# Four time units of slack before a K table's matmul set, in the list schedule of a gated mix kernel

## The chip, the cores and the metric

The kernel runs on one core of a Trainium2 chip. TensorE (PE in the profile) multiplies matrices into PSUM, VectorE (DVE) and ScalarE (ACT) do elementwise work, GpSimd (POOL) and SyncE (SP) mostly issue DMAs. The metric is the device time of one execution in microseconds; lower is better. Every engine works through its own instructions in the order in which the program issues them, and waits at an instruction whose inputs are not there yet.

## The reference

For a sequence u of 2048 tokens with 512 channels, two branches are mixed with a gate per token. Branch A is a long convolution whose kernel K is a sum of 128 complex exponentials per channel; branch B is a bilinear GLU with 1792 hidden units.

```python
g = sigmoid((x * gate_w).sum(-1, keepdims=True))            # x = A_u, [1, 2048, 512]
# A: state-space convolution
P = exp((A * dt[:, None])[:, :, None] * pos[None, None, :]) # [512, 128, 2048]
K = 2.0 * einsum("dn,dnl->dl", C, P).real                   # [512, 2048]
y = irfft(rfft(u_t, 2 * L) * rfft(K, 2 * L), 2 * L)[:, :, :L]
a = y + u * D_skip
# B: bilinear GLU
b = einsum("bsf,fd->bsd", (x @ w_gate) * (x @ w_up), w_down)
out = g * a + (1 - g) * b
```

## The kernel before

The whole computation is written as small tasks that are collected by `work.add` (L198) and then put in order by `Work.run` (L268), a list scheduler. A task has an engine, an expected duration in units of a microsecond, the tiles it reads and writes, a rank, and, for sets of many small matmuls, a value `many`. `Work.inputs` (L227) gives the time at which a task's inputs are there by the plan: the latest planned end of the tasks that it depends on, plus a small lag. `slots` (L236) adds the wait for a free buffer. `run` then picks, again and again, the task with the smallest (start, rank, number) over all engines, fixes its planned start and end, and goes on. The plan's times are used for the order only: on the chip each engine takes its instructions in this order and waits by semaphores for what it needs. Two sets with `many` are planned to start no nearer than `APART` = 6 units (or `LESS` = 4, for the last two groups' transforms) after the end of the set before (L186, L294, L306).

Three streams share the engines.

- The GLU (`glu`, L650). 14 hidden tiles in four groups, over four token tiles of 512. Each product is done with three matmuls (high and low parts), as tasks of three matmuls of 128x512 (`product`, L540, `down`, L583). They have rank 2, the lowest, and fill TensorE wherever nothing else is ready. In the profile they are the matmuls into `pg`, `pu` and `y`.
- The K tables (`phases`, `direct_powers`, `leads`, `x_table`, `v_table`, L892 to L1034). The 512 channels go in 16 blocks of 32. For each block VectorE and ScalarE build an X table (two buffers) and a V table (one buffer) of powers of the complex exponentials. `k_block` (L1041) multiplies them on TensorE in one set of 128 small matmuls (`kgen`, the matmuls `k<-v,x`), which ScalarE and VectorE then fold into the tile `kt`. This set, called a K set below, has rank 0 and `many` = `APART`. The next block's V table may be written only when the K set has read this one.
- The convolution by Fourier transforms. After every fourth block (b % 4 == 3) `k_first` (L1072) transforms the K of 128 channels, one of four groups, and `transforms` (L1338) does the second stage, the product with the transformed u, the inverse and the last stage (`m_second`, `m_product`, `m_inverse`, `m_last`), through DRAM buffers between the stages. Stores of the transformed K (`sk_d`) and of the inverse (`y_d`) are issued on SP's queue, the loads that follow the first on POOL's. All these stages are sets with `many` too. The last group's transforms are what the end of the kernel waits for, beside the last GLU matmuls.

The main loop (L1381) adds, for each block b, the phases of block b + 1, the V table of b, the powers and the X table of b + 1, and the K set of b; the scheduler orders them as it finds them ready.

Of the kernel before, what the change touches and what calls it, by code (L numbers as in the profile page):

```python
# [20 lines left out]
KT = D // P  # L21
# [148 lines left out]
class Work:  # L170
# [24 lines left out]
    def memory(self):  # L195
        return Tile(self, None, None, None, None, None, False)

    def add(self, engine, us, fn, r=(), w=(), rank=1, after=0.0, dma=0, hold=(), rows=(), many=0):  # L198


        task = Task(len(self.tasks), engine, us, fn, rank, after, dma)
        task.rows, task.many = rows, many
        self.tasks.append(task)
        clash = lambda p, q: p is None or q is None or p == q
        split = lambda x: x if isinstance(x, tuple) else (x, None)
        for tile, part in map(split, r):
            task.deps.update(t for p, t in tile.writers if clash(p, part))
        for tile, part in map(split, w):
            task.deps.update(t for p, t in tile.writers + tile.readers if clash(p, part))
        for tile, part in map(split, r):  # L210
            tile.readers.append((part, task))
        for tile, part in map(split, w):
            tile.writers.append((part, task))
        for tile, _ in map(split, [*r, *w, *hold]):
            if tile.pool and tile not in task.tiles:
                task.tiles.append(tile)
                tile.users.append(task)
        task.deps.discard(task)
        return task
# [7 lines left out]
    def inputs(self, task):  # L227

        at = task.after
        for d in task.deps:  # L230
            if d.end is None:
                return None
            at = max(at, self.ready(task, d))
        return at

    def slots(self, task, at):  # L236

# [87 lines left out]
def gated_mix_kernel(  # L325
# [16 lines left out]
    pe, dve, act, sp, pool_q = (InOrder(tc, e) for e in (nc.tensor, nc.vector, nc.scalar, nc.sync, nc.gpsimd))  # L342
    uv = u.rearrange("(p r) d -> p r d", r=NR)
    ov = out.rearrange("(p r) d -> p r d", r=NR)
    work = Work()
    add = work.add
# [12 lines left out]
    m_su, m_sk, m_y, m_out, m_xs, m_turn = (work.memory() for _ in range(6))  # L359
# [5 lines left out]
    def new(pool, tag, shape, dtype=F32, bufs=1, loose=False):  # L365
        return work.tile(pools[pool], tag, shape, dtype, bufs, loose)

    def bank():
        return new("ps_k", "k", [P, D], bufs=4, loose=True)
# [5 lines left out]
    def stage(shape):  # L375
        return new("mid", "ts", shape, bufs=2, loose=True)
# [23 lines left out]
    def power_sets():  # L400
        for k in range(NP):
            pool_q.memset(turns[:, k : k + 1], float(TURNS[k]))

    add("dve", 0.5, memsets, w=[m_const, m_skip], rank=0)
    add("pool", 4.0, power_sets, w=[m_powers], rank=0)


    raws = {}

    def load(key, src, rank=0):  # L410
        if key in raws:
            return
        t = raws[key] = new("glu", "raw", [P, D], bufs=2)
        add("sp", 0.42, lambda: sp.dma_start(t.t, src), w=[t], dma=256, rank=rank)
# [35 lines left out]
    ws, wd, xs = {}, {}, {}  # L450
# [522 lines left out]
    def x_table(b):  # L973

        x, ri, (su, di) = xtab[b], ris[b], sus[b]
        ps = new("tab", "ps", [P, TB, 4])
        lead = [(x, ("l", k)) for k in range(3)]
        tt(0.26, lambda: ps.t, lambda: x.t[:, 0, :, 0:4], lambda: x.t[:, 1, :, 0:4], ALU.add, lead, [ps])
        outer(
            x, lambda: x.t[:, :, :, 0:4], lambda: ps.t, lambda: ri.t[:, :, :, W_M],  # L980
            lambda: su.t[:, :, W_M], lambda: di.t[:, :, 4:11], [*lead, ps, ri, su, di],
        )
        return x
# [54 lines left out]
    def apart_of(q):  # L1038
        return work.LESS if q >= KT - 2 else work.APART

    def k_block(b, x, v):  # L1041
        pk = bank()

        def kgen():
            pv = pk.t.rearrange("p (g j) -> p g j", j=64)
            for d in range(TB):
                ch, g = d % 4, d // 4
                for c in range(2):
                    pe.matmul(
                        pv[32 * ch : 32 * ch + 32, g, :], x.t[:, c, d, :], v.t[:, c, d, :], start=c == 0, stop=c == 1,  # L1050
                        tile_position=(0, 32 * ch),
                    )

        if b % 4 == 0:
            kts["now"] = new("tab", "kt", [P, 2, 2, 32, 16])
        kt, g0 = kts["now"], b % 4 * 8
        add("pe", 2.15, kgen, r=[x, v], w=[pk], rank=0, hold=[kt], many=work.APART)
        pv = lambda a: pk.t.rearrange("p (g a b k) -> p g a b k", a=2, b=2, k=16)[:, :, a]
        side = lambda h: kt.t[:, h, :, g0 : g0 + 8].rearrange("p b g k -> p g b k")
        add("act", 0.37, lambda: act.copy(side(1), pv(0)[:, :, :, ::-1]), r=[pk], w=[(kt, (1, b % 4))])  # L1060
        for h, op in enumerate((ALU.add, ALU.subtract)):
            add(
                "dve", 0.42, lambda h=h, op=op: dve.tensor_tensor(out=side(h), in0=pv(1), in1=side(1), op=op),
                r=[pk, (kt, (1, b % 4))], w=[(kt, (h, b % 4))], rank=0,
            )
        if b % 4 == 3:
            k_first(b // 4, kt)
# [48 lines left out]
    def evict(q, n, us, to, src, r, w):  # L1116

        if q == KT - 1 and n % 2:
            add("dve", us + 0.1, lambda: dve.tensor_copy(to(), src()), r=r, w=w)
        else:  # L1120
            add("act", us, lambda: act.copy(to(), src()), r=r, w=w)
# [92 lines left out]
    def m_inverse(q, T0, ys, ws):  # L1214


        banks, shape = [bank() for _ in range(4)], [P, 2, 2, 2, P]
        if q == KT - 1 and T0:
            sts = [new("tab", n, shape) for n in ("ri", "e")]
        else:  # L1220
            sts = [stage(shape) for _ in range(2)]

        def fn():
            for t in range(2):
                for i in range(2):
                    cs, to = slice(P * i, P * i + P), slice(P * (2 * t + i), P * (2 * t + i) + P)
                    for k in range(2):
                        for e in range(2):
                            for j in range(4):
                                lanes = slice(32 * j, 32 * j + 32)  # L1230
                                pe.matmul(
                                    banks[j].t[64 * e : 64 * e + 64, to], ws[t].t[lanes, i, e, k],
                                    ys[t].t[lanes, k, e, cs], start=k == 0, stop=k == 1, tile_position=(32 * j, 64 * e),
                                )

        add("pe", 2.13, fn, r=[*ys, *ws], w=[*banks, (m_turn, (q, T0))], rank=1, hold=sts, many=apart_of(q))
        for j in range(4):
            st, m = sts[j // 2], j % 2
            evict(
                q, j, 0.6, lambda st=st, m=m: st.t[:, :, :, m],  # L1240
                lambda j=j: banks[j].t.rearrange("p (t i d) -> p t i d", t=2, i=2), [banks[j]], [(st, m)],
            )
        for h in range(2):
            st = sts[h]
            for p in range(2):
                b0 = 32 * (T0 + p) + 16 * h
                add(
                    "sp", 0.42,
                    lambda b0=b0, st=st, p=p: sp.dma_start(
                        y_d[q, b0 : b0 + 16].rearrange("(u e) n d -> (e n) u d", u=8),  # L1250
                        st.t[p::2].rearrange("p t i j d -> p (t i j) d"),
                    ),
                    r=[st], w=[(m_y, (q, T0 + h, p))], dma=256,
                )
# [125 lines left out]
    x = x_table(0)  # L1380
    for b in range(NB):  # L1381
        if b + 1 < NB:
            if b % 2 == 0:
                amplitudes([n for n in (b + 1, b + 2) if n < NB])
            phases(b + 1)
        v, old = v_table(b), x
        if b + 1 < NB:
            direct_powers(b + 1)
            leads(b + 1)
            x = x_table(b + 1)  # L1390
        k_block(b, old, v)
        if b % 4 == 3:
            transforms(b // 4)
# [56 lines left out]
```

## Time and profile before

| | |
|---|---|
| three runs | 592.37, 589.72, 591.31 us; median 591.31 |
| the profiled execution | 588.79 us, its span 587.0 us |
| TensorE | 575.0 us busy, 98% of the span |
| VectorE | 511.7 us, 87% |
| ScalarE | 401.3 us, 68% |
| GpSimd | 113.8 us, 19% |
| the 16 K sets | 2048 matmuls, 33.0 us of TensorE |

The profile is of one execution. A row of a timeline gives the start in us from the span's beginning, the time taken, the engine, the line (here always that of the helper that issues), the operation, the tile written and the tiles read, how many instructions were merged into the row, and in brackets the engine's idle time before it with what ended it. A row of the waits gives who waited for whom, the total in us, how often, and the longest. A row of the groups ends with busy us and mean ns of one, then the idle time before them.

### The profile page before, as it was taken

The page shows a single profiled execution, that of the slowest core. Times are in us where ns is not written, and L with a number is a line of the kernel's source. Part 1 is how long each engine was busy: PE and PEld are TensorE (multiplying, and loading weights), DVE is VectorE, ACT ScalarE, POOL GpSimd, SP SyncE. Part 2 cuts the span into 40 slices and gives each one's busy share as a digit, 9 for nine tenths or more (in the row PEclk, how much of TensorE's full clock was granted, in tenths as well). Part 3 has the DMA queues.
Part 4 walks back from the last instruction along what each step waited for, and adds up shares of the span by engine and source line. Part 5 has one row for each costly group of instructions (what it writes and reads, how often), then busy time and mean ns, then how long its engine had stood idle before and what let it go on. Part 6 is the DMA issues. An engine that isn't in the chain of part 4 may idle for free.

```text
span 587.0 us, 14842 instructions
## 1 busy us (share of the span) xinstructions
PE 575.0 (98%) x5996; PEld 434.4 (74%) x5996; DVE 511.7 (87%) x812; ACT 401.3 (68%) x891; POOL 113.8 (19%) x159
## 2 busy tenths in 40 slices
PE   8899999999999999999999999999899999999996
PEld 5677767788877777787687877867777876777764
DVE  6998999999998999999999999996899982456845
ACT  5358998898679588878877665799587343434351
POOL 0003212411111231310134101112323104202011
PEclk9999999999999999999999999999999999999999
DMA  8999779797767697997789856899959448989887
GB/s 279 400 370 342 268 275 337 197 312 205 194 179 206 198 253 197 233 274 254 173 185 266 188 150 198 174 276 280 216 128 258 76 147 234 274 254 254 261 190 133
DMA packets 71687, 136.28 MB, mean 232 GB/s; under 512 B 6852, under 2 KB 35780, under 8 KB 69188
## 3 DMA queue, kind: packets, MB, share of 16 engines
q1 hardware_dynamic: 47668, 87.10, 43.2%
q0 software_dynamic: 23392, 47.98, 38.8%
q8 instruction: 47, 0.77, 0.5%
q10 hardware_dynamic: 560, 0.26, 0.2%
q14 instruction: 20, 0.16, 0.1%
HBM read 80.27 MB, written 55.05 MB: 231 GB/s over the span
## 4 chain that ended last, share of the span: by engine, by line
PE 89%; DVE 4%; DMA 2%; ACT 2%; issue 1%; DVEq 0%; SPq 0%; ACTq 0%
PE pg L124 25%; PE pu L124 24%; PE y L124 24%; PE k L124 16%; DMA raw<-in_wts 1%; DVE x L124 1%; DVE v L124 1%; DMA y<-in_xT 1%; ACT whi L124 0%; DVE in L124 0%; DMA raw<-in_xT 0%; ACT acc L124 0%; DVE h L124 0%; DVE dlo L124 0%; ACT L124 0%
## 5 line engine op out<-in xcount | busy, mean ns | idle before, releaser
L124 PE MATMUL pg<-xs,whi 128*128 128x512 f32 x448 | 138.9, 391 | 0.3 <-ACT whi L124 0.3
L124 PE MATMUL pu<-xs,whi 128*128 128x512 f32 x448 | 138.3, 390 | 0.0
L124 PEld LDWEIGHTS pg<-xs,whi 128*128 128x128 f32 x448 | 84.3, 188 | 19.0 <-ACT whi L124 1.9
L124 PEld LDWEIGHTS pu<-xs,whi 128*128 128x128 f32 x448 | 84.3, 188 | 17.0
L124 PE MATMUL y<-dhi,hl 128*128 128x512 f32 x224 | 89.5, 400 | 2.8 <-ACT dhi L124 1.7
L124 PE MATMUL pu<-xs,wlo 128*128 128x512 f32 x224 | 90.1, 402 | 0.0
L124 PE MATMUL pg<-xs,wlo 128*128 128x512 f32 x224 | 89.9, 401 | 0.1
L124 PE MATMUL y<-dlo,hh 128*128 128x512 f32 x224 | 87.5, 390 | 2.0 <-issue 1.6
L124 PE MATMUL y<-dhi,hh 128*128 128x512 f32 x224 | 87.2, 389 | 0.0
L124 ACT COPY ev<-k 128x512 f32<-128x512 f32 x112 | 59.2, 598 | 21.6 <-PE k L124 21.6
L124 POOL DMA_DIRECT2D out<-acc x44 | 39.4, 973 | 156.6 <-ACT acc L124 152.7
L124 ACT CAST hh<-h 128x512 fp32r<-128x512 f32 x56 | 34.9, 623 | 44.4 <-DVE h L124 43.9
L124 PEld LDWEIGHTS y<-dhi,hl 128*128 128x128 f32 x224 | 42.0, 188 | 25.4 <-issue 10.6
L124 ACT ACTIVATE acc<-y,ngate 128x512 f32<-128x512 f32 x62 | 42.0, 687 | 27.0 <-PE y L124 22.2
L124 PEld LDWEIGHTS pu<-xs,wlo 128*128 128x128 f32 x224 | 42.0, 188 | 19.5 <-issue 9.5
L124 PEld LDWEIGHTS pg<-xs,wlo 128*128 128x128 f32 x224 | 42.1, 188 | 16.4 <-issue 6.2
L124 DVE TENSOR_TENSOR h<-pu,h 128x512 f32<-128x512 f32 x56 | 38.5, 688 | 17.0 <-PE pu L124 16.2
L124 PEld LDWEIGHTS y<-dhi,hh 128*128 128x128 f32 x224 | 42.0, 188 | 10.7 <-issue 1.8
L124 ACT COPY h<-pg 128x512 f32<-128x512 f32 x56 | 33.0, 588 | 23.2 <-PE pg L124 14.2
L124 PEld LDWEIGHTS y<-dlo,hh 128*128 128x128 f32 x224 | 42.1, 188 | 8.8 <-DVE dlo L124 0.8
L124 DVE TENSOR_TENSOR hl<-h,hh 128x512 fp32r<-128x512 f32 x56 | 38.4, 686 | 3.4 <-ACT hh L124 3.3
L124 POOL DMA_DIRECT2D su_d<-ev x32 | 18.0, 579 | 92.6 <-ACT ev L124 92.6
(130 smaller groups left out, 981.4 us busy)
## 6 DMA issues: line engine op xcount, KB each, us to landing
xs<-xs_d SPq DMA_DIRECT2D x36, 512.0 KB, 5.7
out<-acc POOLq DMA_DIRECT2D x44, 256.0 KB, 5.6
raw<-in_wts SPq DMA_DIRECT2D x33, 256.0 KB, 5.9
xs_d<-xs SPq DMA_DIRECT2D x16, 512.0 KB, 6.1
su_d<-ev POOLq DMA_DIRECT2D x32, 256.0 KB, 7.0
y_d<-ts SPq DMA_DIRECT2D x28, 256.0 KB, 6.3
in<-su_d POOLq DMA_DIRECT2D x12, 512.0 KB, 7.5
sk_d<-ev SPq DMA_DIRECT2D x6, 1024.0 KB, 5.9
```

The lines of the kernel that those rows point to most:

```text
L124: got = getattr(self.engine, name)(*args, **kw)
```

## The change

`add` gets an argument `slack`, kept with the task, and `inputs` adds it to the time at which the task counts as ready. The K sets of blocks 0 to 13 get a slack of 4.0 units, those of blocks 14 and 15 none. The inverse's set is given a slack too, which is 0.0 in both branches, so that nothing changes there.

```diff
-    def add(self, engine, us, fn, r=(), w=(), rank=1, after=0.0, dma=0, hold=(), rows=(), many=0):
+    def add(self, engine, us, fn, r=(), w=(), rank=1, after=0.0, dma=0, hold=(), rows=(), many=0, slack=0.0):
...
-        task.rows, task.many = rows, many
+        task.rows, task.many, task.slack = rows, many, slack
...
             at = max(at, self.ready(task, d))
-        return at
+        return at + task.slack
...
-        add("pe", 2.15, kgen, r=[x, v], w=[pk], rank=0, hold=[kt], many=work.APART)
+        add("pe", 2.15, kgen, r=[x, v], w=[pk], rank=0, hold=[kt], many=work.APART, slack=4.0 if b < 14 else 0.0)
...
-        add("pe", 2.13, fn, r=[*ys, *ws], w=[*banks, (m_turn, (q, T0))], rank=1, hold=sts, many=apart_of(q))
+        add("pe", 2.13, fn, r=[*ys, *ws], w=[*banks, (m_turn, (q, T0))], rank=1, hold=sts, many=apart_of(q), slack=0.0 if q < KT - 1 else 0.0)
```

The slack enters the plan alone: no instruction is added, removed or made to wait for anything new on the chip. What changes is the order in which tasks are issued on each engine.

## The prediction

> **What bounds the kernel now.** I read the page first (busy shares, clock, chain), then the list of waits on TensorE, then the timelines of TensorE and VectorE around the K sets, then the last 15 us.
>
> ```profile
> span 587.0 us, 14842 instructions
> PE 575.0 (98%) x5996; PEld 434.4 (74%) x5996; DVE 511.7 (87%) x812; ACT 401.3 (68%) x891; POOL 113.8 (19%) x159
> PEclk9999999999999999999999999999999999999999
> q8 instruction: 47, 0.77, 0.5%
> PE 89%; DVE 4%; DMA 2%; ACT 2%; issue 1%; DVEq 0%; SPq 0%; ACTq 0%
> ```
>
> TensorE (PE) is busy for 575.0 of 587.0 us, the clock is full in all slices, and 89% of the chain that ended last is PE. The change moves PE work in the issue order and neither adds nor removes any, so it can win only PE's idle time (12.0 us) and lose by making more of it. Its longest waits, and the one that matters here:
>
> ```profile
> PE y L124 <- ACT dhi L124: 1.7, 1, 1.7
> PE y L124 <- issue: 1.6, 1, 1.6
> PE k L124 <- DVE acc L124: 1.5, 1, 1.5
> PE k L124 <- DVE v L124: 0.4, 1, 0.4
> ```
>
> "PE k <- DVE v" is the one wait that the change is aimed at, a K set that stands first in PE's queue while VectorE still finishes its V table: one case in 16 sets, 0.4 us in all. The others end on ScalarE's cast of a weight, on the first memset, or on nothing that the profile shows.
>
> **The change, part by part.** The list schedule now treats a K set of blocks 0 to 13 as ready 4 units after its tables, so it is issued later if it stood closer than that behind them. How close did it stand? The first row of each pair is the last write of the V table on VectorE (DVE), the next the set on PE; for blocks 0, 2, 3 and 12 the third is VectorE's first write to the next block's V table, which has one buffer and must wait for the set. In order: blocks 0, 1, 2, 3, 4, 7, 11, 12, 15.
>
> ```profile
> 98.53 0.62 DVE L124 TENSOR_TENSOR v<-v,sq 128x256 f32<-128x256 f32 x1
> 99.29 2.05 PE L124 MATMUL k<-v,x 128*32 128x64 f32 x128 [0.43 <-DVE v L124]
> 102.33 1.08 DVE L124 TENSOR_TENSOR v<-ri,di 128x896 f32<-128x896 f32 x1
> ...
> 121.46 0.61 DVE L124 TENSOR_TENSOR v<-v,sq 128x256 f32<-128x256 f32 x1
> 123.17 2.04 PE L124 MATMUL k<-v,x 128*32 128x64 f32 x127
> ...
> 141.63 0.64 DVE L124 TENSOR_TENSOR v<-v,sq 128x256 f32<-128x256 f32 x1
> 143.08 2.06 PE L124 MATMUL k<-v,x 128*32 128x64 f32 x128
> 145.50 1.10 DVE L124 TENSOR_TENSOR v<-ri,di 128x896 f32<-128x896 f32 x1
> ...
> 162.41 0.61 DVE L124 TENSOR_TENSOR v<-v,sq 128x256 f32<-128x256 f32 x1
> 163.66 2.07 PE L124 MATMUL k<-v,x 128*32 128x64 f32 x128
> 166.29 1.08 DVE L124 TENSOR_TENSOR v<-ri,di 128x896 f32<-128x896 f32 x1
> ...
> 187.97 0.63 DVE L124 TENSOR_TENSOR v<-v,sq 128x256 f32<-128x256 f32 x1
> 191.34 1.87 PE L124 MATMUL k<-v,x 128*32 128x64 f32 x116
> ...
> 267.24 0.64 DVE L124 TENSOR_TENSOR v<-v,sq 128x256 f32<-128x256 f32 x1
> 268.71 2.06 PE L124 MATMUL k<-v,x 128*32 128x64 f32 x128
> ...
> 373.26 0.63 DVE L124 TENSOR_TENSOR v<-v,sq 128x256 f32<-128x256 f32 x1 [0.28 <-ACT sq L124]
> 380.08 2.07 PE L124 MATMUL k<-v,x 128*32 128x64 f32 x128
> ...
> 405.80 0.62 DVE L124 TENSOR_TENSOR v<-v,sq 128x256 f32<-128x256 f32 x1
> 407.08 2.07 PE L124 MATMUL k<-v,x 128*32 128x64 f32 x128
> 409.20 1.09 DVE L124 TENSOR_TENSOR v<-ri,di 128x896 f32<-128x896 f32 x1 [1.19 <-PE k L124]
> ...
> 476.42 0.64 DVE L124 TENSOR_TENSOR v<-v,sq 128x256 f32<-128x256 f32 x1
> 482.64 2.07 PE L124 MATMUL k<-v,x 128*32 128x64 f32 x128
> ```
>
> Margins (set's start less the table's end): 0.14 us in block 0, 1.10 in 1, 0.81 in 2, 0.64 in 3, 2.74 in 4, 0.83 in 7, 6.19 in 11, 0.66 in 12, 5.58 in 15. Taking a unit as a microsecond, the sets of blocks 0, 1, 2, 3, 4, 7 and 12 are issued later, by 4 less the margin: 3.86, 2.90, 3.19, 3.36, 1.26, 3.17 and 3.34 us. Block 11 is past 4 already and stays unless something before it pushes; 14 and 15 get no slack. What is issued ahead of set 0 is as before, so the first 97 us cannot change.
>
> Term 1, the wait at set 0: some five GLU triples now go ahead of the set, and the 0.43 us go. What is late next is the set itself, not PE: -0.43 us. The bounds are 0 (VectorE is later too) and -0.43.
>
> Term 2, what moves with the set. It issues no DMA. Its evictions (one copy on ScalarE, an add and a subtract on VectorE into the K tile) come 3 us later; behind them waits only the first transform of a group of four blocks (sets 3, 7 and 11), which then carries its store on SP's queue and its load on POOL's with it. PE's own work is the same 128 matmuls per set. I take 0; the cover is the GLU, which fills PE in front of the set instead of behind it. Without it this is the third rival.
>
> Term 3, VectorE. In blocks 0, 2, 3 and 12 it wrote to the next V table 0.99, 0.36, 0.56 and 0.05 us after the set's end, so a later set would hold it back by 2.87, 2.83, 2.80 and 3.29 us, 11.8 us in all, if nothing else could be put in between. But the X table of the next block, which needs another buffer and not this one, is there to be put in between. Each of these groups runs once or twice per block:
>
> ```profile
> L124 DVE TENSOR_TENSOR x<-m,x 128x896 f32<-128x896 f32 x32 | 34.3, 1085 | 0.0
> L124 DVE TENSOR_TENSOR x<-x,su 128x896 f32<-128x896 f32 x16 | 17.4, 1088 | 0.0
> L124 DVE TENSOR_TENSOR m<-ps,ri 128x896 f32<-128x896 f32 x16 | 17.4, 1087 | 0.1
> L124 DVE TENSOR_TENSOR x<-x,di 128x896 f32<-128x896 f32 x16 | 17.4, 1086 | 0.0
> ```
>
> That is 2 x 1.085 + 1.088 + 1.087 + 1.086 = 5.4 us of cover per block against at most 3.3 us, and since the schedule is written by a list that takes whatever is ready, it will take it. I take 0; without the cover +11.8 us on the chain of tables (second rival); a gain is excluded, since VectorE gets no work taken away.
>
> Term 4, the one wait that ends on nothing the profile shows:
>
> ```profile
> 413.21 0.39 PE L124 MATMUL y<-dlo,hh 128*128 128x512 f32 x1 [1.57 <-issue]
> ```
>
> It stands 4 us behind set 12's end, in the middle of a run of GLU matmuls. If its cause is how closely set 12 followed other sets, a set 3.34 us later may lose it (-1.57) or bring another of its kind elsewhere (+1.57). I take 0 and keep both. [...]
>
> Sum: -0.43 us against the profiled execution's 588.79 us (span 587.0 and 1.8 around it), so 588.36. The three timed runs have a median of 591.31, 2.52 above the profiled one; the same 0.43 off the median gives **590.9 us**.
>
> **The rivals.** First, faster: the profiled execution shows a quicker run than the timed ones, and what the others lose, 2.52 us, is PE waiting for tables. Margins of 0.14 to 1.10 us in six blocks (0, 1, 2, 3, 7, 12) are small against an engine that is busy for 87%, so a late VectorE would show at just these sets, and 4 us of distance would hide it. Against it: the profile has one such wait, and nothing shows where other runs lose time. Price: 591.31 - 2.52 - 0.43 = 588.4, and with term 4's stall gone 586.8.
>
> Second, slower, the one mechanism on the other side: the cover of term 3 fails, because the X table's work was placed elsewhere, and VectorE's chain of tables is pushed at sets 0, 2, 3 and 12 by up to 11.8 us. Block 15's set absorbs 5.58 us (its margin). The end absorbs little:
>
> ```profile
> 572.57 1.09 PE L124 MATMUL k<-x,w_t 64*32 64x512 f32 x16
> 577.38 1.28 POOL L124 DMA_DIRECT2D out<-x  x1 [0.19 <-DVE kt L124]
> out<-x POOLq DMA_DIRECT2D x1, 256.0 KB, 7.2
> ```
>
> The last inverse transform is on PE at 572.57; its output goes out at 577.38 and lands 7.2 us later, at 584.6, 2.4 us ahead of the end at 587.0. So 11.8 - 5.58 - 2.4 = 3.8 us, 595.1; it decides from a push of 8 us on. For it: VectorE already waits 1.19 us for set 12.
>
> Third, slower by the sets' order: sets 3 and 7 come 3.36 and 3.17 us later, and with them the transforms of groups 0 and 1. Where these follow each other at the least allowed distance the shift is handed on, past set 11 to group 2, until one of group 2's sets falls behind block 15's. Group 2's third set stood just ahead of it:
>
> ```profile
> 475.22 1.14 PE L124 MATMUL k<-in,w2s 32*32 32x512 f32 x32
> ```
>
> It would cost its 1.14 us and the required 4.0 behind it, 5.1, in the part that ends last, less the 2.4 of room: +2.7, so 594.0 (and 597.8 with the second rival).
>
> Fourth, the change does nothing that can be seen: the sets move and PE neither wins nor loses, 591.3. On the median it cannot be told from the forecast.
>
> **How the numbers follow.** 0.5% is 3.0 us, about what a measurement of this kernel can tell from no change: faster means under 588.35, slower over 594.27. The forecast with the fourth 0.37 (of it 0.02 faster, 0.32 same, 0.03 slower); first rival 0.25 (0.21 faster, 0.04 same); second 0.21 (0.19 slower, 0.02 same); third 0.17 (0.08 same, 0.09 slower, its price lying next to the bound). Together: faster 0.23, same 0.46, slower 0.31. The forecast's own range is 589.0 to 592.9 (terms 1 and 4: -0.43 - 1.57 and +1.57 on 591.31). The range for 8 in 10 reaches to the first rival's full price and beyond the second's: 587.0 to 596.3.
>
> **What would show it.** Term 1: no "PE k <- DVE v" wait, and seven sets 1 to 4 us further behind their tables. Term 3: in blocks 0, 2, 3 and 12 the X table's operations stand ahead of "v<-ri,di", and DVE has no new wait on "PE k"; such waits of 2 to 3 us, and block 15's table ending well after 477, are the second rival. Third: a "k<-in" set of group 2 behind block 15's set. Term 4: the 1.57 us gone, or another "issue" wait of its size. The prediction is wrong if PE's idle time grows by over 3 us, or if the time falls below what 12.0 us of idle time and these terms allow.

## The result, and the profile after

The changed kernel takes 593.91 us (median of 22 runs, 590.58 to 597.28) against 592.33 for the kernel before (22 runs, 589.72 to 593.90): a ratio of 1.0033, 95% interval 1.0017 to 1.0049. So it is slower, by a third of a per cent, where 590.9 and a gain of 0.43 us were forecast. The profiled execution took 595.6 us. From its page, and its list of waits on TensorE:

```profile
span 593.8 us, 14844 instructions
PE 580.1 (98%) x5996; PEld 437.8 (74%) x5996; DVE 512.4 (86%) x812; ACT 400.5 (67%) x891; POOL 113.6 (19%) x159
PEclk9989999999999999999999989999999999999999
```

```profile
PE k L124 <- issue: 2.2, 1, 2.2
PE y L124 <- issue: 2.1, 1, 2.1
PE y L124 <- DVE dlo L124: 1.6, 1, 1.6
PE k L124 <- DVE acc L124: 1.5, 1, 1.5
PE y L124 <- ACT acc L124: 0.7, 1, 0.7
PE pg L124 <- ACT whi L124: 0.6, 1, 0.6
PE y L124 <- ACT dhi L124: 0.5, 1, 0.5
PE pg L124 <- ACT h L124: 0.3, 1, 0.3
PE pg L124 <- issue: 0.3, 1, 0.3
```

The wait that the change was aimed at, "PE k <- DVE v", is gone. In its place stand two stops of 2.2 and 2.1 us that end on "issue", that is on nothing that the profile shows, where before had one of 1.6 and one of 0.2. And two slices have a clock below full, one just behind the first stop and one at 31 us, ahead of anything that the change moved. Here is where the stops lie, in TensorE's timeline of the changed kernel:

```profile
339.16 2.06 PE L124 MATMUL k<-y,w3s 32*64 32x128 f32 x124
343.43 0.43 PE L124 MATMUL k<-y,w3s 32*64 32x128 f32 x4 [2.21 <-issue]
351.79 1.14 PE L124 MATMUL k<-in,w2s 32*32 32x512 f32 x32
...
416.45 2.07 PE L124 MATMUL k<-v,x 128*32 128x64 f32 x128
421.01 0.50 PE L124 MATMUL y<-dlo,hh 128*128 128x512 f32 x1 [2.07 <-issue]
433.29 1.14 PE L124 MATMUL k<-in,w2s 32*32 32x256 f32 x34
```

The first stop cuts a set of 128 matmuls four short of its end; the second comes one matmul after a K set. By the profile no semaphore ended either. What arrived in those moments is in the list of DMA queues, for the windows 341 to 341.9 us and 418.5 to 419.4 us, which both hold this one row of queue 8:

```profile
q8 instruction: 1, 0.02, 6.2%
```

It is a block of instructions. The trace's packets of that queue give 47 of 16,384 bytes in a run, and TensorE has 12,105 recorded instructions (6,109 on its sequencer's and weight-load side, 5,996 matmuls), so some 256 to a block. The block's packet started at 341.01 and 418.55 us, and TensorE went on at 343.43 and 421.01, 2.4 and 2.5 us later. In the profile of before the block started at 410.78 and the stop there ended at 413.21, 2.4 us later as well. So it looks as if TensorE had run out of instructions; the experiments test this.

Shortly behind the first stop the clock was lower. This is TensorE's clock in two stretches of the changed kernel, one in the stop and one shortly behind it (the column before the DMA share is the granted clock):

```profile
341.20:343.40 2.20, 0.02 (x2) 0.00 (x0) 2.17 (x4) 1.38 (x3) 0.87 (x1) 1.00 0.92 263
345.13:348.54 3.41, 3.41 (x10) 2.65 (x9) 0.69 (x1) 2.12 (x4) 0.00 (x0) 0.50 1.08 284
```

For 3.41 us behind the stop the clock was halved, which is 1.7 us more. The half clock in the slice at 31 us lasted 3.41 us as well (31.10 to 34.51, below). What halved it the trace does not show.

### The profile page after: what moved, and what is told of

Read it like the earlier page. It is cut to its first block, busy times and chain, and to the rows that moved or that the text cites. A ratio compares the mean times of both kernels' runs of the same rounds, so it can differ in the third digit from the quotient of the medians.

```text
span 593.8 us, 14844 instructions
## 1 busy us (share of the span) xinstructions
PE 580.1 (98%) x5996; PEld 437.8 (74%) x5996; DVE 512.4 (86%) x812; ACT 400.5 (67%) x891; POOL 113.6 (19%) x159
## 4 chain that ended last, share of the span: by engine, by line
PE 90%; DMA 4%; ACT 2%; issue 2%; DVE 2%; SPq 1%; DVEq 0%; ACTq 0%
PE pg L124 25%; PE y L124 25%; PE pu L124 24%; PE k L124 16%; DMA kt<-in_wts 2%; DMA v<-in_prm 1%; DMA ev<-in_wts 1%; SPq L124 1%; DVE v L124 1%; ACT ev L124 0%; DVE in L124 0%; ACT acc L124 0%; ACT L124 0%; ACT xs L124 0%; ACT h L124 0%
## 5 line engine op out<-in xcount | busy, mean ns | idle before, releaser
L124 PE MATMUL pu<-xs,whi 128*128 128x512 f32 x448 | 140.3, 395 | 0.0
L124 PEld LDWEIGHTS pu<-xs,whi 128*128 128x128 f32 x448 | 85.7, 191 | 17.7
L124 PE MATMUL pg<-xs,wlo 128*128 128x512 f32 x224 | 91.1, 407 | 0.3 <-ACT h L124 0.3
```

What stands on the lines that cost most here:

```text
L124: got = getattr(self.engine, name)(*args, **kw)
```

## The experiments

The theory, called "blocks" below: the changed order is not slower by itself, but its sets of 256 instructions (128 matmuls, 128 weight loads) happen to lie against the edges of the instruction blocks so that TensorE runs dry twice. The K set at 416 us uses up a block's worth of instructions in 2.07 us. That the next block comes late because it is asked for only when the set has begun is the author's guess; no trace shows when it is asked for. The rival, "order": the new order itself costs the time. They can be told apart without touching the order: some tiny matmuls ahead of all real work move the whole program against the edges.

```diff
             for _ in range(2):
                 pe.matmul(scratch.t, zero.t[:, :P], zero.t, start=True, stop=True)
+            for _ in range(16):
+                pe.matmul(
+                    scratch.t[0:32, 0:64], zero.t[:, 0:32], zero.t[:, 0:64], start=True, stop=True, tile_position=(0, 0),
+                )
```

Each of these calls is two weight loads and two matmuls (with 16 calls the page has 6028 of each instead of 5996), so 16 calls shift the program by 64 instructions and 36 by 144. The planned time of the warm-up is left alone, so that the schedule is the same instruction for instruction. The longer warm-up makes the first real matmuls later (the stretch named next began 0.6 us later with 64 instructions and 3.8 with 144, in the order of before); to keep that apart I use, beside the time, the stretch from the first transform set (`k<-in,w2s`, some 40 us into the run) to the end. Its start is a row like these, of before and after:

```profile
37.43 1.11 PE L124 MATMUL k<-in,w2s 32*64 32x512 f32 x16
```

```profile
40.76 1.11 PE L124 MATMUL k<-in,w2s 32*64 32x512 f32 x16
```

The stretch is 587.0 - 37.43 = 549.6 us before and 593.8 - 40.76 = 553.0 us after. The 3.3 us between the two starts lie where both programs are the same instruction for instruction, so the change did not make them. They lie in TensorE's pace. Two windows of before, and the same two of the changed kernel (the first x counts the matmuls):

```profile
7.10:10.60 3.50, 3.50 (x17) 2.89 (x16) 3.29 (x15) 2.60 (x6) 0.00 (x0) 1.00 1.04 393
31.00:34.50 3.50, 3.50 (x17) 2.92 (x16) 3.46 (x7) 1.91 (x4) 0.00 (x0) 1.00 0.86 284
```

```profile
7.10:10.60 3.50, 3.50 (x9) 2.72 (x9) 3.36 (x14) 2.58 (x6) 0.00 (x0) 1.00 1.01 364
31.10:34.51 3.41, 3.41 (x9) 2.63 (x8) 3.40 (x7) 1.24 (x3) 0.00 (x0) 0.50 0.74 211
```

In both, the changed kernel did 9 matmuls where before did 17. In the second its clock was halved; in the first the trace has no record of its clock yet (the first, of a full clock, is at 10.62 us, against 7.10 before).

**The changed kernel and the kernel before, 64 and 144 instructions on.**

> The changed kernel, its order untouched, with 16 tiny matmuls (64 TensorE instructions) put into the warm-up ahead of the first real matmul, so that the same program lies 64 instructions further on against the 256-instruction blocks in which TensorE's instructions arrive. Theory (blocks): the changed kernel is slower because two of its 128-matmul sets (at 339 and 416 us) begin 8 and 17 instructions ahead of a block's edge and TensorE then stands for 2.2 and 2.1 us without instructions; with 64 more, both edges lie well ahead of the sets, both stops go, and with them 4 to 6 us of the profiled 593.8; median 588 to 592, at least as fast as the kernel before. New stops of up to 2 us each can come at other sets (252, 359, 386 us). Rival (order): the new order itself costs it, so the time stays at 593.9 within 1 us, and stops or not, the ratio to the kernel before stays near 1.003.

> The kernel before, order untouched, with the same 64 TensorE instructions ahead. Theory (blocks): its stops at 335 (0.65 us) and 411 us (1.57 us) go or move, so the time changes by 1 to 4 us one way or the other although nothing of the order is touched; stops become likely at sets whose start falls 6 to 56 instructions ahead of an edge (123, 248, 352, 380, 501 us). Rival (order): the time stays within 0.5 us of the kernel before, ratio 1.000 within 0.1%.

> The changed kernel with 36 tiny matmuls (144 instructions) ahead, order untouched. Theory (blocks): by the place of the edges three sets remain at risk (276, 446, 505 us), against five without them, so no stop at 339 or 416 us and a median of 588 to 592. Rival (order): 593.9 within 1 us.

> The kernel before with 144 instructions ahead, order untouched. Theory (blocks): three sets at risk (143, 223, 298 us) against six, so no stop at 335 and 411 us, 1 to 3 us faster than the kernel before, 589 to 591. Rival (order): ratio 1.000 within 0.1%.

| kernel | median us | ratio to before (95%) | stretch us | stops on "issue", us |
|---|---|---|---|---|
| changed, +64 | 588.41 | 0.9948 (0.9928 to 0.9968) | 586.1 - 40.22 = 545.9 | none |
| changed, +144 | 590.79 | 0.9974 (0.9955 to 0.9993) | 588.9 - 42.16 = 546.7 | 0.3 |
| before, +64 | 591.53 | 0.9982 (0.9960 to 1.0003) | 588.0 - 37.98 = 550.0 | 0.5 |
| before, +144 | 596.62 | 1.0090 (1.0064 to 1.0115) | 593.3 - 41.27 = 552.0 | 2.1 |

One of the 12 executions of the changed kernel at +144 took 3249.69 us, which nothing on record explains.

The rival falls: with the same order, the changed kernel is now faster than the kernel before, by 64 instructions that compute nothing, and the order of before becomes slower by 0.9% with 144. Before with 64 settles nothing: its two stops went, one of 0.5 us came at another set, a wait on ScalarE (`ACT acc`) grew from 1.0 to 2.3 us, and the time moved by 0.4 us instead of the 1 to 4 expected, which is about what the rival had. The expectation of 589 to 591 for before with 144 was wrong. Two things were not in it: the long warm-up (its stretch begins 3.8 us later than that of before) and a stop of 2.1 us at the set of block 2, which was on the list of sets at risk. The row, and those of its list of waits that matter:

```profile
152.15 0.73 PE L124 MATMUL pg<-xs,whi 128*128 128x512 f32 x2 [2.07 <-issue]
```

```profile
PE y L124 <- ACT acc L124: 2.3, 2, 1.7
PE pg L124 <- issue: 2.1, 1, 2.1
```

A list of sets at risk is thus no more than that: of the 14 sets listed for these four kernels three stopped, one for 0.3 us.

**A whole block on, and 64 on without the longer warm-up.** With 256 instructions, a block's worth by the count above, every edge is back at the same instruction of the program; if the tiny matmuls worked in any other way, the stops should stay away. The other kernel gives up one of the two large warm-up matmuls for 17 tiny ones (4 instructions less, 68 more).

> The changed kernel with 64 tiny matmuls (256 instructions, one whole block) ahead, order untouched: every edge falls on the same instruction of the program as in the changed kernel itself. Theory (blocks): the stops come back at the inverse's set near 339 and after the K set near 416 us (both some 6 us later by the longer warm-up), 1.5 to 2.5 us each, and the time from the first transform set to the end is 551 to 554 us, as in the changed kernel (553.0), not 546 to 547 as with 64 and 144 instructions. Rival (anything else that the tiny matmuls do, such as a later start against the DMAs): no stop at these two sets, 546 to 547 us.

> The changed kernel shifted by the same 64 instructions without the longer warm-up: one of the two large warm-up matmuls gives way to 17 tiny ones. Theory (blocks): no stop at the two sets, as with 64 instructions; the start is 0 to 1.4 us earlier, so 587 to 588.5 us, 0.993 to 0.996 of the kernel before. Rival (order): 593.9 within 1 us.

With 256 the stops came back, both, at the same two sets (timeline of TensorE):

```profile
343.13 2.06 PE L124 MATMUL k<-y,w3s 32*64 32x128 f32 x124
347.17 0.43 PE L124 MATMUL k<-y,w3s 32*64 32x128 f32 x4 [1.98 <-issue]
353.88 1.14 PE L124 MATMUL k<-in,w2s 32*32 32x512 f32 x32
...
418.55 2.06 PE L124 MATMUL k<-v,x 128*32 128x64 f32 x128
423.11 0.50 PE L124 MATMUL y<-dlo,hh 128*128 128x512 f32 x1 [2.07 <-issue]
```

They stand at the same matmul, four before the set's end and one behind the K set. The stretch is 595.9 - 45.19 = 550.7 us, 4.8 over the 545.9 without stops; a little under what was expected, since here no half clock followed them. This kernel was timed once, at 597.77 us. The shifted kernel without the longer warm-up took 586.86 us, 0.9923 (0.9894 to 0.9951) of before, and in the same two places its timeline reads

```profile
336.19 2.09 PE L124 MATMUL k<-y,w3s 32*64 32x128 f32 x128
344.56 1.14 PE L124 MATMUL k<-in,w2s 32*32 32x512 f32 x32
...
409.22 2.07 PE L124 MATMUL k<-v,x 128*32 128x64 f32 x128
423.69 1.14 PE L124 MATMUL k<-in,w2s 32*32 32x256 f32 x34
```

Since the order is the same, set by set, the rows price the stops. From the inverse's set to the next: 351.79 - 339.16 = 12.63 us in the changed kernel, 353.88 - 343.13 = 10.75 with 256, 344.56 - 336.19 = 8.37 here. So the stop costs 2.4 us and the half clock behind it 1.9 more. From the K set to the next: 433.29 - 416.45 = 16.84 against 423.69 - 409.22 = 14.47, so 2.4 us. A third, small one (0.3 us in the list above) cost 0.5 us at block 1's set. 2.4 + 1.9 + 2.4 + 0.5 = 7.2, and the stretches differ by 553.0 - 545.9 = 7.1 us.

**The change in parts.**

```diff
-slack=4.0 if b < 14 else 0.0
+slack=4.0 if b == 0 else 0.0
```

and `4.0 if 0 < b < 14 else 0.0` in the other kernel.

> Slack 4.0 for block 0's K set alone. My prediction's first term by itself: the 0.43 us wait at set 0 goes. Theory (blocks): the order changes from 97 us on, so the sets fall elsewhere against the blocks' edges; the wait at set 0 is gone or under 0.3 us, and what the time does beyond that (592 within 4 us) is the sum of the stops without a releaser, which the trace shows. Rival (order): 0.4 us under the kernel before, 591.5 within 0.5 us, or, if set 0 is what costs the change its time, 593.9.

> Slack 4.0 for the K sets of blocks 1 to 13, none for block 0. Theory (blocks): the wait of 0.43 us at set 0 is back, and the time follows the stops without a releaser: 589 to 594, with about 546.5 us plus the stops from the first transform set to the end. Rival (order): slower than the kernel before by 1.6 to 2 us, as the change is.

Block 0 alone: 588.74 us, 0.9933 (0.9909 to 0.9958); stretch 584.4 - 37.45 = 546.9 us. The last three rows of its waits:

```profile
PE k L124 <- DVE v L124: 0.4, 1, 0.4
PE y L124 <- DVE dlo L124: 0.3, 1, 0.3
PE pg L124 <- ACT h L124: 0.3, 1, 0.3
```

No "issue" row is left. The 0.4 on "DVE v" stands at the set of block 2 here, not at set 0. The slack of one set moved the time by 3 us, seven times the wait at which it was aimed: TensorE's order differs from that of before in 1231 of 5992 places, from set 0 on, and the two stops of before are gone, 2.4 of the 2.7 us by which the stretch is shorter. The rival's numbers, 591.5 or 593.9, both missed.

Blocks 1 to 13 without block 0: 593.21 us, 1.0029 (0.9998 to 1.0059), which is in both ranges and tells nothing apart. Its stretch, 592.3 - 38.77 = 553.5 us, is more than 546.5 and its one large stop explain:

```profile
463.79 0.73 PE L124 MATMUL pg<-xs,whi 128*128 128x512 f32 x2 [1.49 <-issue]
...
577.48 1.09 PE L124 MATMUL k<-x,w_t 64*32 64x512 f32 x16
```

Its last inverse transform stands 592.3 - 577.48 = 14.8 us ahead of the end, as far as before (587.0 - 572.57 = 14.4); but the GLU had less left, and from TensorE's last matmul, at 583.17, to the end passed 9.1 us. Before, that was 587.0 - 582.05 = 5.0 us (the start of its last matmul). This points to the chain of the last group's transforms setting the end here, by some 4 us, which no other kernel of this study shows; what in its order did it stays open.

**The order of before at other edges, beside the best kernel.**

> The shifted changed kernel once more, beside two shifted kernels with the order of before. No stop without a releaser after the first transform set, 545.9 us from there to the end; 586 to 588 us, 0.991 to 0.996 of the kernel before.

> The order of before, with 27 tiny matmuls in place of one large one in the warm-up (104 instructions on). Three of its sets are at risk (298, 372, 501 us). If none of them stops, theory (blocks): 547.2 us from the first transform set to the end (549.6 less the two stops of 0.65 and 1.75), 1.3 more than the changed order without stops, and 588 to 590 us. Rival (the order of the change is worth nothing by itself): the same time as the shifted changed kernel within 0.5 us.

> The order of before, 200 instructions on in the same way (51 tiny matmuls). Sets at risk: 214, 269, 438 us. The longer warm-up starts the work up to 2 us later. From the first transform set to the end 547.2 us if none stops, else up to 2.4 more for each stop; 588 to 593 us. Rival: as with 104.

| kernel | median us | ratio to before (95%) | stretch us | stops on "issue", us |
|---|---|---|---|---|
| changed, 64 on, short warm-up | 586.30 | 0.9896 (0.9868 to 0.9925) | 584.4 - 38.49 = 545.9 | none |
| before, 104 on | 591.19 | 0.9978 (0.9955 to 1.0002) | 589.5 - 40.45 = 549.0 | none |
| before, 200 on | 598.07 | 1.0089 (1.0057 to 1.0122) | 595.6 - 43.45 = 552.1 | 1.9, 1.6, 0.5 |

At 104 the order of before has no stop left, so its rows price the two stops of before. From the inverse's set to the next: 344.46 - 335.40 = 9.06 us before, 348.09 - 339.68 = 8.41 at 104. From set 12 to the next: 430.10 - 407.08 = 23.02 against 431.99 - 410.73 = 21.26. So 0.65 and 1.76, as the expectation had them. The first of these stops cut the set where it was cut in the changed kernel:

```profile
337.71 0.43 PE L124 MATMUL k<-y,w3s 32*64 32x128 f32 x4 [0.25 <-issue]
```

The stretch at 104 is still 3.1 us longer than the changed order's: not equal, as the rival had it, and more than the 1.3 expected. What its list of waits has that the changed order's has not:

```profile
PE y L124 <- ACT acc L124: 1.8, 2, 1.1
PE k L124 <- DVE v L124: 0.4, 1, 0.4
```

and of the shifted changed kernel, which has no row for "DVE v":

```profile
PE y L124 <- ACT acc L124: 0.7, 1, 0.7
PE pg L124 <- ACT h L124: 0.3, 1, 0.3
```

The wait on an eviction (`acc`) 244 us into the run, 1.1 us, has gone from the changed order, with set 0's:

```profile
244.48 0.50 PE L124 MATMUL y<-dhi,hl 128*128 128x512 f32 x1 [1.06 <-ACT acc L124]
```

In the five traces of before's order the row "ACT acc" comes to 1.0 to 2.3 us, in the six of the changed order to 0.7 each. So the changed order is better by 1 to 4 us where neither stops: 549.6 less before's two stops of 0.65 and 1.75 is 547.2, 1.3 over 545.9, and 549.0 is 3.1 over it; the other three traces of before's order, less the idle time of their stops, are 549.5, 549.9 and 548.1. With 200 on, three stops made the order of before the slowest kernel timed here.

The shifted changed kernel, 586.86 and 586.30 us in its two series of runs, beats the kernel before and the changed one.

**One place for all the stops.** The 13 traces have 14 stops on "issue". Counted in TensorE's recorded instructions (matmuls, weight loads and its sequencer's own), each of them ends when 449 or 450 have started past a multiple of 256, in either order and at every shift. There are 602 such places in the traces, and at none did TensorE go on sooner than 2.19 us after the start of the block's packet. Counted so, the changed kernel's sets at 339 and 416 us begin 7 instructions behind such a place and 2 ahead of one, not 8 and 17 ahead as the expectation had it.

## Why the prediction was wrong

**What bounds the kernel: right, but not how it can lose.** TensorE's time decided. The prediction had the change lose only by more idle time of TensorE. In the profiled pair that grew by 1.7 us, from 12.0 to 593.8 - 580.1 = 13.7, while the same 5996 matmuls kept TensorE busy for 580.1 us instead of 575.0. Of these 5.1 us 3.2 lie ahead of the stretch, where the change did nothing, and 1.9 in it, behind the first stop, where the clock was at 0.50 for 3.41 us.

**Term 1, the wait at set 0: right in kind, small.** "PE k <- DVE v" is gone, and the seven sets named stand 4.3 to 6.8 us behind their tables. Set 0 stands at 106.80, 4.3 us behind the end of its table, the first row here (101.89 + 0.62).

```profile
101.89 0.62 DVE L124 TENSOR_TENSOR v<-v,sq 128x256 f32<-128x256 f32 x1
106.80 2.07 PE L124 MATMUL k<-v,x 128*32 128x64 f32 x128
114.80 1.08 DVE L124 TENSOR_TENSOR v<-ri,di 128x896 f32<-128x896 f32 x1
```

Some of the gain was lost to a 0.3 us wait of the GLU on ScalarE ("PE pg <- ACT h") in the same place.

**Term 3, VectorE: right.** The last row above is the next V table's first product; the X table's operations, from 106.15 on, now stand ahead of it, and it did not wait. The second rival did not come about. Block 15's table was done at 485.44 us, 8.4 us later than before, of which 3.3 are the late start and some 5 the stops ahead of it; its set was issued 1.1 us behind the table instead of 5.6, so the room counted on there was used.

**Term 4: the step that failed.** "I take 0 and keep both" ends of 1.57 us for one stop without a releaser. No run shows the cause that the term supposes, how closely set 12 followed other sets. The runs showed the place of a set against the edges of TensorE's instruction blocks, and more than one such stop. The changed kernel has three such stops, 2.4 + 2.4 + 0.5 us, and a half clock of 1.9 us behind one, 7.2 us in all; before has 0.65 + 1.75 = 2.4. The difference, +4.8 us in the profiled pair, is more than all the rest of the change, and the term had been put at 0. More distance between sets did not take the stop behind set 12 away: the set began 6.27 us behind the end of the set before it, against 4.91 before, and the stop cost 2.4 us instead of 1.75. With the order untouched, 64 instructions ahead took this stop and the first one away, 256 brought both back, and the 64 moved the time of the same order from 593.91 to 588.41 us.

**The sum.** +4.8 for the stops less the 1.3 that the order is worth against the same trace of before is +3.5 us, and the profiled stretches differ by 553.0 - 549.6 = 3.4. The timed medians differ by 1.58, the ratio's interval holding 1.0 to 2.9 us. Of the 22 timed runs of the changed kernel 15 had the granted clock of the profiled one, 0.994, with a median of 594.36 us, and the five at 0.997 one of 591.82. The timed runs of before lose time to a lower clock too (last section), which its profiled run did not; that makes the timed difference smaller. That the timed runs have the same stops at the same sets is not shown by them one by one. Two slips of the prediction change nothing: its own lower bound is 591.31 - 0.43 - 1.57 = 589.3, not 589.0, and block 14's set, 0.50 us behind its table, is a seventh with a small margin.

**First rival.** Its prices of 588.4 and 586.8 us are about what the changed order takes without stops, but its cause was not seen: the five traces of before's order, among them one of 591.22 us at a clock of 0.997, each have 0.4 or 0.5 us of "PE k <- DVE v" and no more, and what the timed runs lose goes with the granted clock (last section). **Third rival.** No set of group 2 fell behind block 15's; its third set, at 470.25 us, stands ahead of it. **Fourth.** The change moved the time beyond its interval.

## What to carry to other kernels

In this kernel, where TensorE is busy for 98%, a change of order was worth 1 to 4 us, and the stops at the edges of its instruction blocks, with a half clock behind one, cost up to 7.2 us: look for idle time on "issue" just behind or within long sets of small matmuls, and try the same order with some instructions more ahead of it, before an order is judged by its time. A stop of that kind is priced by comparing the same sets in two runs of one order; behind one of the nine large stops here the clock was at 0.50 for 3.41 us, which cost 1.9 us more.

## What the runs showed of the hardware

- TensorE went on 2.2 to 3.0 us after its instruction block's DMA packet had started, in all 14 stops; in the three largest of the profiled pair 2.4 to 2.5 us, though the packet itself took 0.9 to 1.0 us. The 47 packets of 16,384 bytes and TensorE's 12,105 recorded instructions make some 256 to a packet.
- The block's packet can start late. Over the 13 traces it started 0 to 298 recorded instructions ahead of the place where the stops end, mostly some 200. In both 2 us stops of the changed kernel, with a set of 256 instructions begun at the edge before, none or one was left. When the blocks are asked for, and why these came late, the traces do not show.
- Of the nine stops of about 1.5 us and more one was followed by 3.41 us at 0.50; the stop of 2.0 us at the same matmul, with 256 instructions ahead, was not. That a stop halves the clock is not shown.
- The spread of the kernel before in its timed runs goes with the granted clock. Its executions beside the experiments with a mean clock of 1.000 took 589.0 to 589.9 us (4 of them), those at 0.996 a median of 592.9 (24) and those at 0.994 a median of 594.5 (6). 0.004 of 590 us at half clock would by this estimate be 4.7 us so spent and 2.4 us lost, about the 2.5 us that the first rival had given to the tables. Where in those runs the clock was halved was not traced; in seven of the 13 traces, one of them before's order at 104 (clock 0.997), it was halved for 3.41 us between 28 and 40 us, ahead of the first K set.
